# Attention and a squared-ReLU layer on one core: sums and copies placed on GpSimd, the last columns in one piece, and a new order

## The chip, the core and the metric

The kernel runs on one core of one Trainium2 chip. A core has TensorE (matmuls, into PSUM banks), VectorE, ScalarE and GpSimd (elementwise work; GpSimd also issues most of the loads) and SyncE (issues stores and transposing DMAs). Each engine works through its own list of instructions in order and waits on semaphores for the others. The metric is the time of one execution in device microseconds (us).

## The reference

The inputs are q, k and v with 4 batches, 8 heads, 768 positions and 64 columns each, and the weights w_in (512 x 2048) and w_out (2048 x 512).

```python
scores = scale * np.matmul(q, k.transpose(0, 1, 3, 2))
is_global = pos[None, :] < 8
is_local = (rel >= 0) & (rel < 96)          # rel = row - column
scores = scores - slopes[h] * dist          # dist: distance, 96 for a global far column
scores = np.where(is_global | is_local, scores, -1e9)
a = softmax(scores)                          # over the columns
x = np.matmul(a, v)                          # (4, 8, 768, 64) -> (3072, 512)
out = (np.maximum(x @ w_in, 0) ** 2) @ w_out # (3072, 512), float32
```

## The kernel before, in words

**Tiles.** The 3072 rows are 24 tiles j of 128 rows, six to a batch. Since a row sees only 96 columns back and the 8 global ones, tile j needs k and v of tiles j and j-1 only; the global rows are copied into 8 rows of tile j-1's k and v that the window does not reach (`gk.j`, `gv.j`: emit_gk at line 719, emit_gv at line 791; read by tile j+1). For each tile: load q, k, v; transpose q and k (`tr` on TensorE and `T` as its copy out of PSUM for the first 8 tiles, a transposing DMA from SyncE, also `T`, for the later ones); scores `sc`; `exp` on ScalarE; the product with the bias table `mul` on VectorE; `pv` (two halves); `norm` (reciprocal and product, VectorE); and the transpose of x, `xT`.

**Blocks.** Two tiles make one of 12 blocks of 256 rows. The first layer is done directly for blocks 0 and 1 (`s1`, then `relu` and `sq`). From block 2 on it is done with seven products instead of eight (`h.blk.g.p1` to `p7`, line 938; g is one of two halves of w_in's 2048 columns), which need sums of operands:

- `isum.i.g` (i 0 to 3, line 881): sums of parts of w_in, 128 x 1024, made once, by VectorE, and kept where the first q and k tiles lay. isum.1 reads isum.0; product p5 reads isum.0, p6 isum.1, p3 isum.2, p7 isum.3.
- `xs.blk.i` (i 0 to 2, line 905): sums of parts of xT, the first 128 x 512, the others 128 x 256, three for each block, by VectorE. xs.0 serves p5 and p7, xs.1 serves p6, xs.2 serves p4.
- `u` copies a running product out of PSUM, `c` adds it to another product in PSUM and applies the ReLU, `q` squares (lines 938 to 1030).

The second layer is done directly for block 0 (`s2.0.s.sub`) and with seven products from block 1 on (`s2.blk.p1.g` and so on, line 1202). These need `wsum.i.g` (line 1126: sums of parts of w_out, 128 x 1024, made once; wsum.1 reads wsum.0, wsum.3 reads wsum.1; product p5 reads wsum.0, p6 wsum.1, p7 wsum.2, p4 wsum.3) and `sum.blk.i` (line 1159: sums of the hidden layer). `part` copies a product out of PSUM, `o` adds the last ones (in fin, line 1272), `st` stores. In the last block the product p3 and its `o` are cut in two, 192 and 64 columns (line 1197), each part with a store of its own.

**Loads.** Loads of q, k, v and of the weights are issued by GpSimd (swdge, line 304; issue lines L307 and L311 in the profile). The first 6 tiles and all weights are `ld` words of the order (ld.win.s.c for w_in's piece s, ld.wout.s for w_out's). From tile 6 on, `load.j` issues v, q and k of tile j. A `gate.j` is a one-element memset on VectorE that collects the waits of VectorE's side for a load into a buffer used before. GpSimd's list holds nothing else but the iota at the start.

**The order.** It is not made by the program at run time: the string ORDER (line 57) lists every step by name, with its PSUM banks behind a colon and its engine behind `@` (A ScalarE, V VectorE). Plan.run takes the words one by one and emits each step, so that each engine's list is the order of its words. Costs and due times in the calls of plan.op are not used in the run.

```python
for word in ORDER.split():
    word, _, banks = word.partition(":")
    name, _, letter = word.partition("@")
    name, _, nth = name.partition("#")
    o = byname[name][int(nth or 1) - 1]
    o["engine"] = self.ENGINES[letter] if letter else next(iter(o["engines"]))
```

In this text a step's place on TensorE is told as the amount of TensorE work that stands in front of it in the order: the sum of its matmuls' start-to-start steps (a product `h` is 0.45 us, half a product `s2` 0.44), counted from the first transpose.

Of the kernel before, what the change touches and what calls it, by code (L numbers as in the profile page):

```python
# [22 lines left out]
class Plan:  # L23


    ENGINES = {"A": "ACT", "V": "DVE"}
# [31 lines left out]
tr.0.0:0 T.0.0@A tr.1.0:1 T.1.0@A bias.0.0:23 sc.0.0 exp.0.1.0 ld.q.1 ld.k.1 exp.0.0.0 tr.0.1:4 tr.1.1:5 ld.v.0  # L58
bias.1.0:6701 T.0.1@A ld.k.2 pv.0.1:3 pv.0.0:2 T.1.1@A sc.1.0 norm.0.0 exp.1.1.0 norm.0.1 ld.q.2 tr.1.2:4 gk.1@V
tr.0.2:5 exp.1.0.0 T.0.2@V bias.2.0:2375 T.1.2@A sc.2.0 E0.0 ld.v.1 exp.1.0.1 pv.1.0:6 exp.1.1.1 ld.q.3 tr.0.3:4  # L60
ld.k.3 E0.1 pv.1.1:0 exp.2.0.0 exp.2.1.1 norm.1.0 ld.v.2 exp.2.1.0 tr.1.3:1 T.1.3@A exp.2.0.1 ld.win.6.0 gv.1@V
trx.0:2 ld.q.4 norm.1.1 ld.k.4 T.0.3@V gk.2@V ones.6 pv.2.0:6 sc.3.0:5304 norm.2.0 pv.2.1:1 xT.0@V norm.2.1 trx.1:7
ld.v.3 tr.0.4:6 ld.win.3.0 trx.2:2 exp.3.1.1 ld.win.4.0 ld.q.5 xT.1@V s1.0.6:4 gk.3@V gv.2@V exp.3.1.0 tr.1.4:1
exp.3.0.0 mul.3.0 exp.3.0.1 mul.3.1 pv.3.0:3 T.1.4@V xT.2@V pv.3.1:7 T.0.4@A ld.k.5 norm.3.0 sc.4.0:5061 exp.4.0.0
exp.4.1.0 s1.0.3:2 s1.0.3#2 norm.3.1 trx.3:3 gv.3@V s1.0.4:5 exp.4.1.1 xT.3@V s1.1.6:7 ld.v.4 relu.0.6@A relu.0.4@V
ld.win.2.0 tr.1.5:0 mul.4.0 tr.0.5:1 exp.4.0.1 ld.win.2.1 sq.0.4@A s1.1.4:3 gk.4@V T.0.5@A pv.4.0:4 s1.0.2:6
ld.win.0.0 sq.0.6@V T.1.5@V relu.0.3@A sc.5.0:5102 relu.1.4@A mul.4.1 s1.0.2#2 pv.4.1:3 norm.4.0 exp.5.1.0 norm.4.1
ld.win.0.1 s1.0.2#3 exp.5.0.1 ld.v.5 gv.4@V s1.0.2#4 sq.1.4@V s1.0.0:4 s1.1.2:1 relu.1.2@A s1.0.0#2 trx.4:0 ld.win.5.0
exp.5.0.0 s1.0.0#3 s1.0.0#4 ld.win.7.0 ld.win.1.0 s1.1.0:3 gate.11 sq.0.3@V mul.5.0 exp.5.1.1 s1.1.3:1 mul.5.1
pv.5.0:5 xT.4@A pv.5.1:2 relu.0.0@V gate.9 s1.1.5:0 s1.0.7:4 load.6 norm.5.0 sq.1.2@A relu.1.3@A norm.5.1 relu.0.2@A  # L70
sq.0.2@A s1.0.1:1 isum.0.0 ld.wout.4 sq.0.0@A relu.0.7@V ld.wout.0 isum.3.1 sq.1.3@A ld.wout.1 ld.wout.2 sq.0.7@V
relu.1.5@A s1.0.1#2 trx.5:5 xT.5@A xs.2.0 h.2.1.p1:6 s1.1.7:2 tr.0.6:4 relu.0.1@A s1.1.1:0 T.0.6@V sq.0.1@A tr.1.6:5
sq.1.5@V relu.1.6@A ld.wout.3 ld.wout.5 relu.1.0@A ld.wout.7 h.2.0.p1:1 u.2.1.1@V relu.1.1@A ld.wout.6 sq.1.6@A
relu.1.7@A u.2.0.1@A sq.1.7@A sq.1.1@A gate.10 sq.1.0@A isum.3.0 h.2.0.p2:4 h.2.1.p2:7 isum.1.0 gate.12 load.8
s2.0.0.0:3 s2.0.0.1:0 load.7 s2.0.1.1 s1.0.5:2 relu.0.5@A xs.2.1 isum.0.1 isum.1.1 isum.2.1 s2.0.2.1 h.2.0.p6 s2.0.1.0
u.2.0.2@A c.2.1.c11 xs.2.2 sum.1.0 T.8 isum.2.0 s2.0.2.0 c.2.0.c11 sq.0.5@A s2.0.3.1 sum.1.2 h.2.1.p6 s2.0.4.1
h.2.0.p7 T.1.6@A s2.0.5.1 s2.0.3.0 wsum.0.0 s2.1.p2.0:7 wsum.0.1 u.2.1.2@A sum.1.1 h.2.0.p5:2 s2.0.6.1 h.2.1.p7
u.2.1.3@A h.2.1.p5:5 q.2.1.c11@V c.2.1.c22 gate.13 s2.0.4.0 u.2.0.3@A q.2.1.c22@A s2.0.5.0 c.2.0.c22 wsum.1.0 wsum.1.1
load.9 q.2.0.c11@A s2.1.p1.0:4 s2.0.7.1 h.2.0.p4 s2.1.p1.1 s2.0.6.0 o.0.1@A c.2.0.c21@A h.2.0.p3 q.2.0.c22@A
q.2.0.c21@A h.2.1.p4 wsum.2.0 s2.0.7.0 wsum.3.1 st.0.1 part.1.p1@A tr.0.7:0 h.2.1.p3 wsum.2.1 sum.1.3 o.0.0@A  # L80
c.2.1.c21@A s2.1.p6.0 c.2.1.c12 c.2.0.c12 s2.1.p6.1 T.0.7@A tr.1.7:1 part.1.p6@A q.2.1.c21@A T.1.7@V s2.1.p2.1
q.2.0.c12@A s2.1.p7.0 st.0.0 s2.1.p7.1 o.1.p2 q.2.1.c12@A sc.6.0:360521 load.10 wsum.3.0 part.1.p7@V s2.1.p5.0 gk.7@A
s2.1.p5.1 s2.1.p4.0 s2.1.p4.1 sum.2.0 exp.6.0.0 s2.2.p1.0:3 o.1.p5 exp.6.1.0 exp.7.0.0 o.1.p4@A mul.6.0 pv.6.1:6
pv.6.0:0 exp.7.1.0 exp.7.1.1 s2.1.p3.0 s2.2.p1.1 T.9 exp.7.0.1 sum.2.1 norm.6.0 load.11 mul.7.0 mul.7.1 norm.6.1
part.2.p1@A sc.8.0:4501 exp.8.0.0 s2.1.p3.1 pv.7.0:2 exp.8.1.1 norm.7.0 s2.2.p6.0 pv.7.1:4 norm.7.1 gk.8@V exp.8.1.0
gv.7@V trx.6:6 s2.2.p6.1 exp.8.0.1 xT.6@A s2.2.p2.0:1 mul.8.0 mul.8.1 trx.7:2 xT.7@A xs.3.0 o.1.p3 sc.9.0:5046
exp.9.0.0 s2.2.p2.1 h.3.0.p1:2 xs.3.1 exp.9.1.0 h.3.1.p1:5 sum.2.2 exp.9.0.1 pv.8.0:7 norm.8.0 xs.3.2 h.3.1.p2:0
u.3.1.1@A h.3.0.p2:4 h.3.1.p6 c.3.1.c11 u.3.0.1@A exp.9.1.1 o.2.p2 part.2.p6@A h.3.0.p5:7 c.3.0.c11 h.3.0.p6 pv.8.1:6
u.3.1.2@A load.12 mul.9.1 s2.2.p5.0 u.3.0.2@A gate.14 T.10 gv.8@A h.3.1.p7 q.3.0.c11@A norm.8.1 load.13 h.3.0.p7
u.3.0.3@A mul.9.0 pv.9.1:0 s2.2.p5.1 h.3.1.p5:4 pv.9.0:6 s2.2.p7.0 u.3.1.3@A st.1.0 q.3.1.c11@A s2.2.p7.1 c.3.0.c22  # L90
h.3.0.p3 part.2.p7@A norm.9.0 q.3.0.c22@A gv.9@V h.3.1.p4 c.3.1.c22 q.3.1.c22@A c.3.0.c12 h.3.1.p3 o.2.p5 c.3.1.c12
gk.9@V norm.9.1 s2.2.p4.0 c.3.1.c21@A h.3.0.p4 T.11 q.3.0.c12@A sum.2.3 q.3.1.c12@A s2.2.p4.1 sum.3.0 sc.10.0:6754
exp.10.0.0 gate.15 sum.3.1 s2.3.p1.0:0 s2.3.p1.1 s2.2.p3.0 exp.10.1.0 xT.8 mul.10.0 o.2.p4@A s2.2.p3.1 part.3.p1@A
sum.3.2 h.4.0.p1:6 exp.10.1.1 s2.3.p6.0 s2.3.p6.1 exp.10.0.1 mul.10.1 pv.10.0:7 part.3.p6@A T.12 xT.9 q.3.1.c21@A
norm.10.0 gk.10@V h.4.0.p2:3 u.4.0.1@A o.2.p3 pv.10.1:4 norm.10.1 s2.3.p7.0 c.3.0.c21@A s2.3.p7.1 st.1.1 xs.4.0
h.4.1.p1:5 sc.11.0:7124 xs.4.1 c.4.0.c11 q.3.0.c21@A h.4.0.p6 gv.10@V xs.4.2 u.4.1.1@A h.4.1.p6 exp.11.1.0 T.13
u.4.0.2@A s2.3.p2.0:3 u.4.1.2@A exp.11.1.1 s2.3.p2.1 xT.10 q.4.0.c11@V sum.3.3 o.3.p2 h.4.1.p2:1 c.4.1.c11 exp.11.0.0
exp.11.0.1 mul.11.0 h.4.0.p7 h.4.1.p7 u.4.0.3@A mul.11.1 h.4.0.p5:4 c.4.0.c22 q.4.1.c11@A h.4.1.p5:7 pv.11.0:1 st.2.0
s2.3.p5.0 u.4.1.3@A c.4.1.c22 norm.11.0 h.4.0.p4 pv.11.1:2 gate.16 part.3.p7@A s2.3.p5.1 h.4.1.p4 q.4.0.c22@A
q.4.1.c22@A c.4.1.c21@A s2.3.p4.0 norm.11.1 c.4.0.c21@A s2.3.p4.1 o.3.p5 h.4.0.p3 h.4.1.p3 xT.11 c.4.0.c12 s2.3.p3.0  # L100
o.3.p4@A s2.3.p3.1 q.4.1.c21@A load.15 c.4.1.c12 q.4.1.c12@A q.4.0.c12@V o.3.p3 q.4.0.c21@A sc.12.0:125604 exp.12.0.0
st.2.1 T.15 s2.4.p1.0:7 s2.4.p1.1 exp.13.0.0 load.14 sum.4.0 sum.4.1 xs.5.0 h.5.1.p1:3 h.5.0.p1:1 st.3.0 exp.12.1.0
h.5.1.p2:5 part.4.p1@A u.5.0.1@A u.5.1.1@A exp.13.1.0 xs.5.1 h.5.0.p2:2 mul.12.0 c.5.0.c11 s2.4.p6.0 h.5.0.p6
q.5.0.c11@A s2.4.p6.1 gk.13@A pv.12.0:2 pv.12.1:6 exp.13.1.1 c.5.1.c11 h.5.1.p6 h.5.0.p5:5 u.5.0.2@A part.4.p6@A
s2.4.p2.0:4 xs.5.2 s2.4.p2.1 u.5.1.2@A norm.12.0 exp.13.0.1 h.5.0.p7 mul.13.0 pv.13.0:2 u.5.0.3@A gate.18 norm.12.1
sum.4.2 mul.13.1 c.5.0.c22 q.5.1.c11@A h.5.1.p7 s2.4.p7.0 o.4.p2 h.5.1.p5:6 q.5.0.c22@A norm.13.0 gate.20 u.5.1.3@A
h.5.0.p4 h.5.0.p3 pv.13.1:0 s2.4.p7.1 c.5.0.c21@A h.5.1.p4 gv.13@A c.5.0.c12 T.14 norm.13.1 c.5.1.c22 s2.4.p5.0
q.5.0.c21@A sum.4.3 q.5.1.c22@V xT.12 s2.4.p5.1 gate.17 sc.14.0:2150 q.5.0.c12@A h.5.1.p3 part.4.p7@A c.5.1.c12
gk.14@V exp.14.0.0 exp.14.0.1 o.4.p5 exp.14.1.0 mul.14.0 s2.4.p4.0 exp.14.1.1 xT.13 s2.5.p1.0:2 h.6.0.p1:5 mul.14.1
q.5.1.c12@A s2.4.p4.1 o.4.p4@A s2.4.p3.0 c.5.1.c21@A sum.5.0 u.6.0.1@A xs.6.0 s2.4.p3.1 sc.15.0:6107 o.4.p3 load.16  # L110
xs.6.1 sum.5.1 h.6.1.p1:3 exp.15.1.1 s2.5.p1.1 exp.15.0.0 pv.14.0:4 norm.14.0 h.6.0.p6 pv.14.1:7 h.6.0.p5:6
part.5.p1@A s2.5.p6.0 s2.5.p6.1 exp.15.0.1 T.16 gate.21 q.5.1.c21@A gv.14@V u.6.0.2@A h.6.0.p2:0 h.6.0.p7 gk.15@V
u.6.1.1@A st.3.1 h.6.1.p6 load.18 mul.15.1 norm.14.1 exp.15.1.0 u.6.0.3@A xs.6.2 c.6.0.c11 sum.5.2 sc.16.0:4710
part.5.p6@V mul.15.0 h.6.0.p4 exp.16.0.0 s2.5.p7.0 c.6.0.c22 load.17 exp.16.1.0 s2.5.p7.1 pv.15.0:4 exp.16.0.1
c.6.0.c21@A part.5.p7@A mul.16.0 pv.15.1:7 exp.16.1.1 norm.15.0 s2.5.p2.0:1 s2.5.p2.1 o.5.p2 h.6.0.p3 norm.15.1
mul.16.1 q.6.0.c11@A c.6.0.c12 h.6.1.p2:5 s2.5.p4.0 u.6.1.2@A gv.15@A q.6.0.c21@A sum.5.3 st.4.0 xT.14 h.7.0.p1:4
h.7.1.p1:0 T.18 q.6.0.c22@A h.6.1.p7 u.6.1.3@A s2.5.p5.0 c.6.1.c11 gate.19 q.6.0.c12@A gk.16@A s2.5.p5.1 o.5.p5
h.6.1.p5:7 c.6.1.c22 s2.5.p4.1 pv.16.0:6 norm.16.0 pv.16.1:5 norm.16.1 h.6.1.p4 h.6.1.p3 c.6.1.c12 s2.5.p3.0 s2.5.p3.1
# [1309 lines left out]
```

## Time and profile before

| | us |
|---|---|
| median of three runs (198.21 to 198.69) | 198.6 |
| the profiled execution, whole | 198.07 |
| its span, from the first to the last instruction of the program | 196.3 |
| TensorE busy / VectorE / ScalarE / GpSimd | 189.2 / 172.4 / 162.9 / 75.1 |
| first matmul of the program's work (the transpose of tile 0) | 4.58 |
| last matmul's end | 192.93 |
| landing of the last store | 195.29 |

TensorE's granted clock is full throughout. Of the instructions' groups by line: L686 is `mul`, L774 and L775 `norm`, L884 `isum`, L918 `xs`, L946 `h`, L991 `c`, L1011 `q` on ScalarE, L1128 `wsum`, L1163 `sum`, L1208 `s2` from block 1 on, L1283 `o`, L1335 `s2` of block 0. L430 and L432 are the copies of ScalarE and of VectorE, whatever they copy. A line of the timeline has the start, the time from the first start to the last end, the engine, the line, the operation, output and inputs with their sizes, the count, and in brackets how long the engine had been idle and what ended it. A group's line has the busy time and the mean of one in ns, then the idle time before. GpSimd's DMA_DIRECT2D is the issue of a load, not its transfer.

### The profile page before, as it was taken

The numbers are of one execution on the slowest core, as the hardware profiler recorded it, in microseconds if no ns is written. First come the engines' busy times: TensorE is split into PE (matmuls) and PEld (weight loads), VectorE is DVE, ScalarE is ACT, GpSimd is POOL, SyncE is SP. The second block draws the span as 40 slices with busy tenths as digits, with TensorE's granted clock in tenths as the row PEclk, the third lists the DMA queues.
The fourth block names the chain that finished last, engine by engine and source line by source line (L and its number), as shares of the span: only waits on it lengthen the run. The fifth ranks groups of instructions, "written<-read, shape, count | busy, mean of one in ns | idle before, by whom it ended". The sixth has DMA issues, their size and how long they took to land.

```text
span 196.3 us, 6770 instructions
## 1 busy us (share of the span) xinstructions
PE 189.2 (96%) x2768; PEld 168.7 (86%) x2768; DVE 172.4 (88%) x426; ACT 162.9 (83%) x335; POOL 75.1 (38%) x93
## 2 busy tenths in 40 slices
PE   7897999999999999999999999999999999999993
PEld 3766999867889989989989999999888999999982
DVE  8188889999989999989999999998999989889772
ACT  6895879966989988979999999889787889878740
POOL 8998895665465309050542085054000000000000
PEclk9999999999999999999999999999999999999999
DMA  8999999999999999989999999999915242034032
GB/s 127 149 157 175 171 187 184 205 186 155 156 182 135 224 129 152 166 108 180 157 128 185 162 97 143 173 158 152 174 33 188 53 62 84 0 30 164 0 134 80
DMA packets 111856, 26.91 MB, mean 137 GB/s; under 512 B 103378, under 2 KB 109010, under 8 KB 111826
## 3 DMA queue, kind: packets, MB, share of 16 engines
q0 software_dynamic: 80256, 13.37, 90.0%
q1 hardware_dynamic: 31570, 13.11, 33.9%
q8 instruction: 21, 0.34, 0.7%
q14 instruction: 9, 0.07, 0.1%
HBM read 27.26 MB, written 6.29 MB: 171 GB/s over the span
## 4 chain that ended last, share of the span: by engine, by line
PE 89%; POOL 5%; DMA 4%; DVE 1%; issue 1%; DVEq 0%; POOLq 0%
PE bank L1208 34%; PE bank L946 32%; PE bank L1057 7%; PE bank L595 5%; PE bank L744 5%; DMA qk_first<-in_q_dram 4%; PE bank L1335 4%; POOL qk_first L307 3%; POOL v L307 1%; PE bank L505 1%; PE bank L812 1%; DVE at L686 0%; POOL win L307 0%; DVE o L1283 0%; POOL early L368 0%
## 5 line engine op out<-in xcount | busy, mean ns | idle before, releaser
L661 ACT ACTIVATE esc<-bank 128x512 bf16<-128x512 f32 x78 | 42.4, 608 | 5.0 <-PE bank L595 4.8
L1011 ACT ACTIVATE hs<-hr 128x512 bf16<-128x512 f32 x71 | 43.3, 635 | 2.5 <-DVE hr L991 1.8
L1208 PE MATMUL bank<-wsum,hsum 128*128 128x256 bf16 x264 | 36.2, 273 | 0.0
L991 DVE CUSTOM_DVE_ANT_0 hr<-bank,early 128x512 f32<-128x512 f32 x45 | 30.6, 687 | 5.2 <-PE bank L946 2.1
L1208 PEld LDWEIGHTS <-hsum 128*128 128x128 bf16 x360 | 32.2, 98 | 3.2
L946 PEld LDWEIGHTS <-qk_first 128*128 128x128 bf16 x480 | 29.4, 98 | 1.6
L946 PEld LDWEIGHTS <-win 128*128 128x128 bf16 x480 | 29.6, 98 | 1.0
L430 ACT COPY early<-bank 128x512 f32<-128x512 f32 x43 | 24.8, 594 | 6.0 <-PE bank L946 5.7
L311 POOL DMA_DIRECT2D v<-in_v_dram x18 | 15.9, 884 | 34.8 <-ACT hs L1011 13.2
L1208 PEld LDWEIGHTS <-hs 128*128 128x128 bf16 x264 | 24.5, 98 | 3.1
L686 DVE TENSOR_TENSOR at<-esc,E 128x1024 bf16<-128x1024 bf16 x39 | 26.1, 683 | 0.3 <-ACT esc L661 0.3
L1208 PE MATMUL bank<-wout,hs 128*128 128x256 bf16 x176 | 24.5, 273 | 0.0
L311 POOL DMA_DIRECT2D qk<-in_q_dram x18 | 15.9, 883 | 22.1 <-DMA qkT<-qk 16.8
L946 PE MATMUL bank<-xs,qk_first 128*128 128x128 bf16 x320 | 22.8, 219 | 0.0
L946 PE MATMUL bank<-xT,win 128*128 128x128 bf16 x320 | 22.6, 219 | 0.0
L775 DVE TENSOR_TENSOR x<-bank,rs 128x256 bf16<-128x256 f32 x48 | 20.4, 425 | 1.7
L861 ACT ACTIVATE hr<-bank 128x512 f32<-128x512 f32 x33 | 19.1, 598 | 2.1 <-PE bank L1057 1.3
L744 PE MATMUL bank<-v,at 128*128 128x65 bf16 x352 | 17.5, 193 | 0.3 <-DVE v L432 0.2
L1283 DVE TENSOR_TENSOR o<-bank,part 128x256 f32<-128x256 f32 (+2 forms) x34 | 14.0, 414 | 3.2 <-PE bank L1208 3.0
L311 POOL DMA_DIRECT2D qk<-in_k_dram x18 | 16.1, 892 | 1.0 <-DMA wout<-in_moe_w_out_dram 0.8
L744 PEld LDWEIGHTS <-at 128*128 128x128 bf16 x352 | 15.0, 98 | 1.7 <-DVE at L686 0.4
L1057 PE MATMUL bank<-xT,win 128*128 128x256 bf16 (+1 forms) x160 | 16.0, 251 | 0.0
(85 smaller groups left out, 340.9 us busy)
## 6 DMA issues: line engine op xcount, KB each, us to landing
out_dram<-o SPq DMA_DIRECT2D x22, 256.0 KB, 4.3
v<-in_v_dram POOLq DMA_DIRECT2D x24, 128.0 KB, 6.0
qk<-in_q_dram POOLq DMA_DIRECT2D x18, 128.0 KB, 6.0
qk<-in_k_dram POOLq DMA_DIRECT2D x18, 128.0 KB, 6.4
wout<-in_moe_w_out_dram POOLq DMA_DIRECT2D x8, 256.0 KB, 9.0
win<-in_moe_w_in_dram POOLq DMA_DIRECT2D x6, 256.0 KB, 6.9
qk_first<-in_q_dram POOLq DMA_DIRECT2D x5, 128.0 KB, 4.6
qk_first<-in_k_dram POOLq DMA_DIRECT2D x5, 128.0 KB, 4.6
```

Of the source, the lines that this page charges most:

```text
L311: nc.gpsimd.dma_start(out=dst, in_=src)
L430: nc.scalar.copy(dst, src)
L661: nc.scalar.activation(out=tiles[tag, j, g][:, odd], in_=tiles.pop(("sc", j, odd, g)).rearrange("p a c -> p (a c)"), func=Act.Exp, scale=s ...
L686: nc.vector.tensor_mul(at, tiles.pop(("esc", j, g)), bias)
L744: nc.tensor.matmul(out=po[:, hi, :], lhsT=tiles["at", j, g][:, odd, at * P : (at + 1) * P], rhs=v_sb[kj][:, h, :], start=(i == 0), stop=(i ...
L775: nc.vector.tensor_tensor(out=x[:, 4 * hf : 4 * hf + 4, :], in0=po[:, :, :D], in1=rs.to_broadcast([P, 4, D]), op=Alu.mult,)
L861: nc.scalar.activation(dst, src, Act.Relu)
L946: nc.tensor.matmul(out=tiles["h", blk, g, bank][:, n], lhsT=left_[:, s, k], rhs=right_[:, k], start=opens and n == 0 and k == 0, stop=k == ...
L991: nc.vector._custom_dve(TENSOR_ADD_SAT, out=hr, in0=src, in1=tiles.pop(("u", blk, g, i)), s0=float("inf"), s1=0.0,)
L1011: nc.scalar.activation(hs, hr, Act.Square)
L1057: nc.tensor.matmul(out=hT[:, c, cols], lhsT=w_in_sb[s][:, kt, c * P : (c + 1) * P], rhs=tiles["xT", blk][:, kt, cols], start=(kt == 0), st ...
L1208: nc.tensor.matmul(out=tiles["acc", blk, bank][:, cols], lhsT=left_[:, s], rhs=right_[:, cols], start=first and s == 0, stop=s == NSTEP - ...
```

## The change

A letter P for GpSimd is added. `isum`, `xs`, `wsum` and `gv` may be placed there. In the new ORDER isum.0.0, isum.0.1, wsum.0.1, wsum.1.1, wsum.2.0, wsum.2.1, 25 of the 30 xs and 10 of the 16 gv are (the other 6 gv are on ScalarE). VectorE keeps isum.1.x, 2.x and 3.x, wsum.0.0, 1.0, 3.0 and 3.1, and xs.2.0, 2.1, 7.0, 9.0 and 9.2. Some copies and squares change between ScalarE and VectorE: VectorE takes 8 more `part`, 7 more squares, 2 more `relu`, 3 more `u` and one more `xT`; ScalarE takes 3 more `gk`. The last block's p3 is no longer cut in two. All words of ORDER stand in a new sequence, the `ld` words too.

```diff
-    ENGINES = {"A": "ACT", "V": "DVE"}
+    ENGINES = {"A": "ACT", "V": "DVE", "P": "POOL"}
...
+    def tensors(e):
+        return nc.gpsimd if e == "POOL" else nc.vector
+
     def any_copy(e, dst, src):
         if e == "ACT":
             nc.scalar.copy(dst, src)
+        elif e == "POOL":
+            nc.gpsimd.tensor_copy(dst, src)
...
-                    nc.vector.tensor_tensor(out=first_sum[i][:, h], in0=x, in1=y, op=op)
+                    tensors(e).tensor_tensor(out=first_sum[i][:, h], in0=x, in1=y, op=op)
...
-                    ("isum", i, g), {"DVE": 0.6}, emit_isum,
+                    ("isum", i, g), {"DVE": 0.6, "POOL": 1.7}, emit_isum,
...
-            nc.vector.tensor_tensor(out=dst, in0=x, in1=y, op=Alu.subtract)
+            tensors(e).tensor_tensor(out=dst, in0=x, in1=y, op=Alu.subtract)
...
-                nc.vector.tensor_tensor(
+                tensors(e).tensor_tensor(
                     out=w_sum[i][:, h],
...
-            cuts = [slice(0, LASTCUT), slice(LASTCUT, HN)] if last and name == "p3" else [slice(0, HN)]
+            cuts = [slice(0, HN)]
```

The part of the new ORDER with the sums of the weights (the old one had all of them on VectorE):

```diff
+relu.0.3@A sc.5.0:7305 s1.0.2:1 ld.wout.0 ld.win.5.0 ld.wout.3 s1.0.2#2 ones.6 relu.1.4@V trx.4:6 sq.1.6@A s1.0.2#3
+sq.0.3@V ld.wout.1 relu.0.0@V s1.0.1:2 s1.0.2#4 xT.4@V exp.5.1.1 exp.5.0.1 ld.wout.2 mul.5.1 gv.4@A exp.5.1.0 load.6
+ld.wout.4 load.7 isum.0.0@P E0.1 h.2.0.p1:5 exp.5.0.0 mul.5.0 s1.0.1#2 s1.1.2:0 pv.5.1:6 pv.5.0:3 h.2.0.p2:7 sq.1.4@A
+sq.0.0@V relu.0.1@A s1.1.1:2 relu.1.2@V sq.0.1@A isum.0.1@P norm.5.0 ld.wout.5 ld.wout.6 sq.1.2@V relu.1.3@A sq.1.3@A
+s1.1.7:0 s1.1.5:4 u.2.0.1@A relu.1.1@A relu.1.5@A relu.0.2@V norm.5.1 gate.10 gate.9 sq.1.1@V h.2.1.p1:3 h.2.1.p2:1
+trx.5:2 xT.5@A sq.1.5@A isum.3.0@V c.2.0.c11 isum.1.0@V u.2.1.1@A s2.0.0.0:6 s2.0.0.1:4 xs.2.0@V q.2.0.c11@A sq.0.2@A
+xs.2.1@V s2.0.1.1 s1.1.0:7 relu.1.0@A ld.wout.7 wsum.2.0@P s2.0.1.0 isum.1.1@V h.2.0.p6 u.2.0.2@A sq.1.0@A c.2.1.c11
...
+h.2.0.p4 h.2.1.p7 c.2.0.c21@A h.2.1.p5:7 s2.0.5.1 q.2.0.c22@A wsum.0.1@P wsum.1.1@P q.2.0.c21@V u.2.1.3@A wsum.2.1@P
...
+c.2.1.c21@A o.0.1@A sum.1.3 T.1.7@A s2.0.5.0 q.2.1.c22@V h.2.1.p3 T.0.7@A c.2.1.c12 wsum.3.1@V s2.0.6.0 s2.0.7.0
+s2.1.p1.0:2 s2.1.p1.1 sc.6.0:034571 o.0.0@A s2.1.p2.0:6 s2.1.p2.1 q.2.1.c12@A part.1.p1@A s2.1.p6.0 s2.1.p6.1
+q.2.1.c21@A load.10 sum.1.2 sum.2.0 exp.6.0.0 exp.6.1.0 exp.7.0.1 exp.7.1.1 s2.2.p1.0:0 mul.6.0 pv.6.1:3 s2.2.p1.1
```

The loads in the order of their issue, before and after (w is a piece of w_in, o of w_out; w0 and w2 come in two halves; a number stands for q, k or v of that tile; from 6 on a `load` is v, q, k):

```
before: q1 k1 v0 k2 q2 v1 q3 k3 v2 w6 q4 k4 v3 w3 w4 q5 k5 v4 w2 w2 w0 w0 v5 w5 w7 w1 load.6 o4 o0 o1 o2 o3 o5 o7 o6 load.8 load.7 load.9
after:  q1 k1 q2 k3 k2 q3 v0 v1 w6 v2 k4 q4 v3 w3 w4 q5 k5 v4 w0 w0 w2 w2 w1 w7 v5 [gv.3] o0 w5 o3 o1 o2 load.6 o4 load.7
        [isum.0.0] [isum.0.1] o5 o6 o7 [wsum.2.0] [xs.2.2] load.8 load.9 [wsum.0.1] [wsum.1.1] [wsum.2.1] load.10 load.11 [xs.3.0] ...
```

## The prediction, as it was put on record

> **What bounds it now.** I read the page's busy shares and slices first, then the chain of waits, then TensorE's matmuls one by one, then the waits and the timeline of GpSimd.
>
> ```profile
> PE 189.2 (96%) x2768; PEld 168.7 (86%) x2768; DVE 172.4 (88%) x426; ACT 162.9 (83%) x335; POOL 75.1 (38%) x93
> PE   7897999999999999999999999999999999999993
> POOL 8998895665465309050542085054000000000000
> PE 89%; POOL 5%; DMA 4%; DVE 1%; issue 1%; DVEq 0%; POOLq 0%
> ```
>
> TensorE is below nine tenths only in the first four slices and the last; the chain that ended last is 89% TensorE. Laid end to end by their start-to-start steps, the matmuls after 17.1 us leave one hole over 0.2 us (0.24 at 140.4). So the time is TensorE's work plus the hole in front of it plus the tail; GpSimd is idle for most of the span, but it issues all loads. The change takes no TensorE work away (eight matmuls of 192 and eight of 64 columns become eight of 256: 0.02 us). It can gain only before 17 us, at the tail, and at that hole. It can lose wherever TensorE comes to wait.
>
> VectorE is near its limit at 30 to 60 us (9.28, 9.41 and 9.30 us busy in each ten), so a wait there is hardly made good.
>
> **The loads.** The timeline of GpSimd at 28 to 38 us carries the most:
>
> ```profile
> 28.72 0.70 POOL L307 DMA_DIRECT2D wout<-in_moe_w_out_dram  x1 [0.32 <-DMA win<-in_moe_w_in_dram]
> 30.05 0.71 POOL L307 DMA_DIRECT2D wout<-in_moe_w_out_dram  x1 [0.63 <-DMA win<-in_moe_w_in_dram]
> 31.90 0.70 POOL L307 DMA_DIRECT2D wout<-in_moe_w_out_dram  x1 [1.14 <-DMA win<-in_moe_w_in_dram]
> ...
> 35.62 0.87 POOL L311 DMA_DIRECT2D v<-in_v_dram  x1 [0.61 <-DMA wout<-in_moe_w_out_dram]
> 36.87 0.87 POOL L311 DMA_DIRECT2D qk<-in_q_dram  x1 [0.38 <-DMA wout<-in_moe_w_out_dram]
> 38.15 0.87 POOL L311 DMA_DIRECT2D qk<-in_k_dram  x1 [0.41 <-DMA wout<-in_moe_w_out_dram]
> ```
>
> These issues wait for a transfer: load n is issued 0.28 us after load n-8 has landed (28.43 then 28.72, 35.33 then 35.62). The program has eight semaphores for such loads, and the changed program waits for them in the same way. Landings are evenly spaced: about 0.85 us for a piece of q, k or v, 1.3 for a weight piece of 256 KB, 0.7 for a half piece. The first 22 loads are the same set in both kernels, in another order, so the 22nd lands at 26.28 in both. From there the changed list gives win 1 27.6, win 7 28.9, v5 29.8, wout 0 31.1, win 5 32.4, wout 3 33.7, wout 1 35.0.
>
> *First loads: -0.2.* Only the first 17 us have holes, and loads 1 to 22 bring no more by then. In the changed order s1.0.1 stands after 18.8 us of TensorE work and needs win 1 (27.6). Before, TensorE had that much work behind it at 27.85. Gain at most 0.2, whatever the first tiles save.
>
> **Two sums of w_in on GpSimd: +1.75.** GpSimd works in order. isum.0.0 stands behind load.7, its k piece the 37th load, which waits for the 29th (wout 1, 35.0): issue 35.25, done 36.13 (0.88 as in the rows above). Only then can the sum begin. VectorE's isum.1.0 needs it and comes up in VectorE's order after 25.9 us of TensorE work (34 to 36 us); xs.2.0 and xs.2.1 queue behind it there; TensorE's h.2.0.p6 needs all three.
>
> A sum on GpSimd is not in this trace. Nearest rows:
>
> ```profile
> L884 DVE TENSOR_TENSOR qk_first<-win 128x1024 bf16<-128x1024 bf16 x2 | 1.4, 682 | 0.0
> L918 DVE TENSOR_TENSOR xs<-xT,xs 128x256 bf16<-128x256 bf16 x20 | 5.7, 284 | 0.3
> L918 DVE TENSOR_TENSOR xs<-xT 128x512 bf16<-128x512 bf16 x10 | 4.2, 416 | 0.0
> L432 DVE COPY v<-v 8x520 bf16<-8x520 bf16 x11 | 3.5, 322 | 0.0
> L368 POOL IOTA early<- 128x256 int32 x1 | 0.3, 333 | 0.4 <-POOLq L1409 0.4
> ```
>
> From below VectorE's 0.68 us. GpSimd's only computing row, the iota, takes 1.30 ns a column for one stream: 1.33 us for 1024 columns, 2.66 if the two operands are read one after the other; that is my upper end. I take 2.0, the middle of GpSimd's own two; for 512 and 256 columns 1.0 and 0.65, for the copy of v 0.7.
>
> isum.0.0 then ends at 38.1, and isum.1.0 (0.62 apart when back to back), xs.2.0 (0.36) and xs.2.1 (0.28) at 39.4. h.2.0.p6 stands after 28.5 us of TensorE work; before, that was reached at 37.65. TensorE is 1.75 us behind (the 0.2 is in this); with 0.68 it is 0.4, with 2.66 it is 2.4.
>
> (The Trainium skill, GPSIMD Engine Reference, section "Performance versus the Vector engine", gives 4497 ns for 2048 float32 columns. Half of it, 2.25 us as an estimate for 1024, would make this term 2.0 and the next 1.7. No run here shows it yet.)
>
> **Four sums of w_out on GpSimd: +1.05.** On GpSimd follow isum.0.1 (to 40.1), three wout issues (0.71 each, 42.3), wsum.2.0 (44.3), xs.2.2 (44.9), load.8 and load.9 (six by 0.88, 50.2), wsum.0.1 (52.2), wsum.1.1 (54.2). VectorE, which also waited for isum.0.1 until 40.1, has 13.9 us by rows from there to wsum.3.1, 12.7 at its back-to-back pace: it arrives at 52.8 and waits for wsum.1.1 until 54.2. Behind it stand sum.1.2, sum.2.0 and mul.6.0, which ends 2.5 us later, at 56.7. TensorE comes to pv.6.1 16.25 us after h.2.0.p6, at 55.65, and stalls 1.05. At 1.7 a sum this is nothing; at 2.66 it is 3.9.
>
> **Twenty-five sums of x: +0.3.** GpSimd makes the pair xs.0 and xs.1 in 1.65 instead of 0.70, 0.95 more. Before, the pair was ready 0.12 to 0.34 us ahead of product p6 in blocks 4, 6, 7 and 11. The new order moves p6 away from the last pv of its block: 8.0 us of TensorE work instead of 6.2 in block 11, 8.5 for 7.0 in 6, 9.4 for 8.5 in 7, 9.2 for 7.4 in 5, 10.7 for 8.9 in 10. That covers it, except in block 4 (8.5 for 9.8) and block 9 (7.6 for 7.4). In block 8 load.21, which waits for the transpose of tile 18, stands ahead of xs.8.0. I put 0.3 on all; between nothing and 2.
>
> **Ten copies of v: 0.** A pv of tile j and the next tile's pv that reads the copy stand at least 1.7 us of TensorE work apart (tile 20); GpSimd needs 0.7, 1.4 if it reads and writes in turn. What would lie late then is pv.21.0.
>
> **Moves between ScalarE and VectorE: 0.** By the rows VectorE loses 16.7 us (25 xs 8.0, six sums 4.1, eleven v copies 3.5, three k copies 0.9, the split 0.2) and takes 12.0 (8 part, 7 squares, 2 relu, 3 u, one xT); ScalarE loses 10.1. Both stay below TensorE. They hid before behind 100% TensorE and do so now; if not, the first to be late are the `c` sums, which left p3 0.13 us.
>
> **The last 256 columns: -0.2.** Now 192 columns are added in 0.36 (192.97), 64 more by 193.46, and two stores go out at 193.35 and 193.78, the last landing at 195.29. One addition of 0.42 ends at 193.4, one store follows and takes 1.65 to 1.75 as its like do: 195.1.
>
> **The sum.** 1.75 + 1.05 + 0.3 - 0.2 = +2.9. On the profiled execution (198.07, span 196.3) that is 201.0. The three runs shown have their median at 198.6, 0.5 above it, so I forecast **201.5**.
>
> **Rivals.**
>
> *The port.* One row speaks of GpSimd and VectorE in each other's way:
>
> ```profile
> 14.10 1.02 POOL L307 DMA_DIRECT2D qk_first<-in_q_dram  x1
> 14.40 0.72 DVE L432 COPY qkT<-qkT 128x32 bf16<-128x32 bf16 x1
> 17.09 0.17 DVE L432 COPY qkT<-qkT 128x32 bf16<-128x32 bf16 x1
> ```
>
> The held copy ends when the GpSimd issue does (15.12); alone it takes 0.17. VectorE's additions of two SBUF operands (0.67 to 0.69 in all 39 `mul` products) are not held by issues. If GpSimd's sums hold those, GpSimd's 12 us of large sums and 19 us of xs each keep VectorE from its two-operand work, 80 of its 168 us. At 30 to 60 us, where VectorE is 93% busy, some 4 us of it reach TensorE, and a little in each block: 206. Against it: no row shows it. (The Trainium skill, SBUF — State Buffer, section "Who interferes with whom", says this: a VectorE instruction with two SBUF inputs contends with a GpSimd one that reads SBUF, the loser waiting to the end. The held copy agrees with its rule for copies; its rule for sums no run here shows.)
>
> *Short sums.* At 0.7 to 1.2 us TensorE is behind by 0.4 to 0.9 only, and the tail takes back 0.2: 199.0.
>
> *Faster.* isum.0.0 is done before VectorE asks for it. It decides at 36.3: then h.2.0.p6 has its operands by 37.65. The last issue ahead would have to end near 34.3, so wout 1 land at 33.1, not 35.0, and wsum.1.1 be done by 53. Then only gains stay: 0.2 first loads, 0.2 tail, 0.2 hole at 140 us: 197.5, as a median 198.0. For it speaks that VectorE is freed of 4.7 us; against it the steady spacing of landings.
>
> *The reordered loads bring nothing*: they land no earlier for the work that needs them. At 0.2 us this is already in the sum.
>
> **Chances.** Forecast 0.50 (200 to 204), port 0.17, short sums 0.11, faster 0.16, no difference (the gains and half a stall cancel) 0.06. A measurement tells some 0.3% (0.6 us) apart: faster 0.16, same 0.06, slower 0.78. Sums at 2.66 give 205 to 206; the range 198.5 to 206 leaves out the faster case and some of the port's.
>
> **What would show it.** isum.0.0 starts at 36 us and VectorE idles before isum.1.0, released by GpSimd; TensorE has a hole of 1.5 to 2 us before h.2.0.p6 near 38 us and one near 56; a dense TensorE after 60. Wrong, if no hole stands near 38 us, if the GpSimd sums last under 1.3 us or over 2.7, if VectorE's `mul` products last longer than 0.69, or if holes gather later, ahead of p6.

## The result, and the profile after

The changed kernel takes 220.12 us (median; 217.53 to 225.54), the kernel before 198.41 on the same chips: ratio 1.107, 95% interval 1.103 to 1.111. The ratio leaves out the one run in the slow state, 225.54. The profiled execution of the changed kernel took 219.96 us with a span of 218.2, against 196.3 before. Line numbers after are 4 higher than before from `exp` on (L690 is `mul`, L888 `isum`, L922 `xs`, L950 `h`, L1017 `q` on VectorE, L1132 `wsum`, L1167 `sum`), and one lower for the loads (L306, L310).

The page of the changed kernel: busy times, the slices of TensorE, of GpSimd and of TensorE's clock, and the chain by engine.

```profile
PE 195.5 (90%) x2760; PEld 170.9 (78%) x2760; DVE 188.5 (86%) x402; ACT 155.6 (71%) x317; POOL 119.5 (55%) x134
PE   7989998079289999979989899998999999999993
POOL 8998958997971077195186476808641126021000
PEclk9999999658969999999999999999999999999999
PE 51%; DVE 17%; POOL 13%; DMA 13%; issue 3%; ACT 1%; DVEq 0%; POOLq 0%
```

TensorE's row has two deep breaks, at slices 8 and 11 (a slice is 5.5 us), and shallow ones later; the clock's row drops in the deep ones and just behind them. The chain is only half TensorE now. VectorE was to lose 4.7 us of work by its rows and shows 16.1 us more.

TensorE's own timeline, around the two breaks (in brackets: how long it had been idle, and what ended that):

```profile
36.98 0.59 PE L1339 MATMUL bank<-wout,hs 128*128 128x512 bf16 x2
44.97 1.86 PE L950 MATMUL bank<-xs,qk_first 128*128 128x128 bf16 x16 [7.39 <-DVE xs L922]
...
61.01 1.01 PE L950 MATMUL bank<-xT,qk_first 128*128 128x128 bf16 x8 [5.18 <-DVE hr L995]
```

The first is h.2.0.p6, where the forecast had a hole of 1.75 us; it is 7.39. The second is h.2.0.p3. VectorE's timeline says why:

```profile
34.89 0.68 DVE L995 CUSTOM_DVE_ANT_0 hr<-bank,early 128x512 f32<-128x512 f32 x1
38.35 4.11 DVE L888 TENSOR_TENSOR qk_first<-qk_first,win 128x1024 bf16<-128x1024 bf16 x1 [2.78 <-POOL qk_first L888]
42.38 0.41 DVE L922 TENSOR_TENSOR xs<-xT 128x512 bf16<-128x512 bf16 x1
42.83 2.08 DVE L922 TENSOR_TENSOR xs<-xT,xs 128x256 bf16<-128x256 bf16 x1
...
51.73 3.58 DVE L1167 TENSOR_TENSOR hsum<-hs 128x1024 bf16<-128x1024 bf16 x1 [0.91 <-ACT hs L1098]
55.34 2.49 DVE L1167 TENSOR_TENSOR hsum<-hsum,hs 128x1024 bf16<-128x1024 bf16 x1
57.75 2.60 DVE L1132 TENSOR_TENSOR wsum<-wout,wsum 128x1024 bf16<-128x1024 bf16 x1
```

isum.1.0 begins at 38.35, when isum.0.0 is there, as foreseen. Then it lasts 4.11 us instead of 0.68, and xs.2.1 lasts 2.08 instead of 0.28. The three sums at 51.73 to 60.35 take 2.5 to 3.6 us each; TensorE's second wait is for the `c` that stands behind them on VectorE. These five take 14.9 us; alone they take 3.0. GpSimd's timeline beside them:

```profile
35.29 0.88 POOL L310 DMA_DIRECT2D qk<-in_k_dram  x1 [0.40 <-DMA wout<-in_moe_w_out_dram]
36.18 4.20 POOL L888 TENSOR_TENSOR qk_first<-win 128x1024 bf16<-128x1024 bf16 x2
40.32 2.16 POOL L306 DMA_DIRECT2D wout<-in_moe_w_out_dram  x3
42.50 2.26 POOL L1132 TENSOR_TENSOR wsum<-wout 128x1024 bf16<-128x1024 bf16 x1
...
52.60 2.15 POOL L1132 TENSOR_TENSOR wsum<-wout 128x1024 bf16<-128x1024 bf16 x1
54.82 2.46 POOL L1132 TENSOR_TENSOR wsum<-wout,wsum 128x1024 bf16<-128x1024 bf16 x1
```

Each long VectorE sum lies over a GpSimd sum. Four of the five end shortly behind its end: xs.2.1 at 44.91, 0.15 us behind wsum.2.0 (44.76); the sum of 51.73 at 55.30, 0.56 behind wsum.0.1 (54.74); the two after it 0.55 behind the next two. The fifth, isum.1.0, ends 2.08 us behind isum.0.1; the last section comes back to it. Operations that read PSUM (`c`, `norm`, `o`) lie over GpSimd sums too and keep their 0.68, 0.42 and 0.42 us.

What GpSimd's work itself takes, in its groups (busy us, mean ns of one, idle before):

```profile
L922 POOL TENSOR_TENSOR xs<-xT,xs 128x256 bf16<-128x256 bf16 x18 | 15.5, 860 | 3.8 <-DVE xs L922 1.9 <-DVE rs L778 0.8
L434 POOL COPY v<-v 8x520 bf16<-8x520 bf16 x10 | 6.4, 639 | 15.3 <-PE bank L748 15.3
L888 POOL TENSOR_TENSOR qk_first<-win 128x1024 bf16<-128x1024 bf16 x2 | 4.2, 2128 | 0.0
```

Where TensorE lost 22 us, by its starts against the work ahead of them in the order: 7.4 in the first break, 2.6 at half clock behind it, 5.3 in the second, 1.7 at half clock behind that, 5.0 spread over blocks 3 to 11; 0.2 was gained before 30 us.

### The profile page after: what moved, and what is told of

It reads as the page before. It is cut to its first block, busy times and chain, and to the rows that moved or that the text cites. A ratio compares the mean times of both kernels' runs of the same rounds, so it can differ in the third digit from the quotient of the medians.

```text
span 218.2 us, 6750 instructions
## 1 busy us (share of the span) xinstructions
PE 195.5 (90%) x2760; PEld 170.9 (78%) x2760; DVE 188.5 (86%) x402; ACT 155.6 (71%) x317; POOL 119.5 (55%) x134
## 4 chain that ended last, share of the span: by engine, by line
PE 51%; DVE 17%; POOL 13%; DMA 13%; issue 3%; ACT 1%; DVEq 0%; POOLq 0%
PE bank L1212 23%; PE bank L950 20%; DMA xT<-x 6%; DVE hsum L1167 5%; DMA wout<-in_moe_w_out_dram 4%; POOL qk_first L306 3%; POOL xs L922 3%; DMA win<-in_moe_w_in_dram 3%; PE bank L599 3%; PE bank L748 3%; PE bank L1339 2%; DVE hr L995 2%; POOL v L306 2%; DVE at L690 2%; DVE qk_first L888 2%
## 5 line engine op out<-in xcount | busy, mean ns | idle before, releaser
L1015 ACT ACTIVATE hs<-hr 128x512 bf16<-128x512 f32 x65 | 40.2, 637 | 12.5 <-DVE hr L995 12.4
L950 PEld LDWEIGHTS <-qk_first 128*128 128x128 bf16 x480 | 31.0, 100 | 18.2 <-issue 11.6
L1212 PE MATMUL bank<-wsum,hsum 128*128 128x256 bf16 x264 | 37.5, 273 | 0.7 <-ACT early L432 0.7
L432 ACT COPY early<-bank 128x512 f32<-128x512 f32 x39 | 22.5, 585 | 17.2 <-PE bank L950 16.8
L950 PE MATMUL bank<-xs,qk_first 128*128 128x128 bf16 x320 | 24.2, 223 | 10.5 <-DVE xs L922 7.4
L922 POOL TENSOR_TENSOR xs<-xT 128x512 bf16<-128x512 bf16 x7 | 9.1, 1294 | 42.9 <-DMA xT<-x 21.6
L950 PEld LDWEIGHTS <-win 128*128 128x128 bf16 x480 | 29.8, 98 | 1.6 <-ACT early L432 0.3
L690 DVE TENSOR_TENSOR at<-esc,E 128x1024 bf16<-128x1024 bf16 x39 | 27.5, 716 | 2.4 <-ACT esc L665 2.2
L950 PE MATMUL bank<-xT,win 128*128 128x128 bf16 x320 | 23.1, 219 | 0.0
L1167 DVE TENSOR_TENSOR hsum<-hs 128x1024 bf16<-128x1024 bf16 (+1 forms) x24 | 19.5, 821 | 1.5 <-ACT hs L1098 0.9
L310 POOL DMA_DIRECT2D v<-in_v_dram x18 | 16.3, 906 | 8.2 <-DVE hsum L1167 6.1
L310 POOL DMA_DIRECT2D qk<-in_q_dram x18 | 16.1, 892 | 3.7 <-DMA qkT<-qk 1.8
L922 POOL TENSOR_TENSOR xs<-xT,xs 128x256 bf16<-128x256 bf16 x18 | 15.5, 860 | 3.8 <-DVE xs L922 1.9
L950 PE MATMUL bank<-xT,qk_first 128*128 128x128 bf16 x160 | 12.4, 223 | 5.2 <-DVE hr L995 5.2
```

Of the source, the lines that this page charges most:

```text
L310: nc.gpsimd.dma_start(out=dst, in_=src)
L432: nc.scalar.copy(dst, src)
L690: nc.vector.tensor_mul(at, tiles.pop(("esc", j, g)), bias)
L922: tensors(e).tensor_tensor(out=dst, in0=x, in1=y, op=Alu.subtract)
L950: nc.tensor.matmul(out=tiles["h", blk, g, bank][:, n], lhsT=left_[:, s, k], rhs=right_[:, k], start=opens and n == 0 and k == 0, stop=k == ...
L1015: nc.scalar.activation(hs, hr, Act.Square)
```

## The experiments

**Theory A**, formed from these lines: while GpSimd makes a sum, VectorE's instructions with two SBUF operands stand still; TensorE waits for them, and the long waits cost it its clock too. **Theory B**, the forecast's: TensorE waits because GpSimd's results come late. **Theory C**: the new sequence and the moves between ScalarE and VectorE cost it, wherever the sums are made. Each kernel ran beside the kernel before on one chip.

**All of GpSimd's steps on VectorE (e1_all_v).**

```diff
-isum.0.0@P ... xs.3.0@P ... gv.9@P (41 words)
+isum.0.0@V ... xs.3.0@V ... gv.9@V
```

> The changed kernel with all 41 steps of GpSimd given to VectorE, at their places in the order: the new order, loads and last piece alone. Theory A (VectorE's instructions with two SBUF operands are held while GpSimd's sums run, and TensorE's two long waits that follow also cost it its clock): without sums on GpSimd no VectorE sum lasts over 0.75 us, the holes before h.2.0.p6 (7.4 us) and h.2.0.p3 (5.2 us) go, the granted clock is 1.000 throughout; VectorE has 12 us more work than before, which may cost a little: 198 to 202 us. Theory B (the forecast's: TensorE waits because GpSimd makes the sums late, in its queue behind the loads): also 198 to 202, since no one waits for GpSimd; but VectorE's sums were never held. Theory C (the new order itself is bad, whoever makes the sums): above 212, with long holes at the same steps.

Measured: 211.32 us, 1.068 of before (1.062 to 1.074). All sums are back at 0.68 us and both breaks are gone, but the time is far above what A and B expected; nor is it C's, which had it above 212 with long holes at the same steps. The waits of TensorE, the largest first:

```profile
PE bank L1212 <- DVE o L1287: 2.2, 1, 2.2
PE bank L950 <- DVE hr L995: 2.0, 2, 1.4
```

With the start's 1.2 us it waits 9.6 us in all for VectorE, in short waits. VectorE has 182.4 us of work here, 10.0 more than before; by this run's rows 15.6 of it are the steps put back (25 xs 8.1, six sums 4.1, ten copies 3.4).

**Only the weights' sums (e2_weights_v), or only the xs (e3_xs_v), back on VectorE.**

```diff
-isum.0.0@P isum.0.1@P wsum.2.0@P wsum.0.1@P wsum.1.1@P wsum.2.1@P
+isum.0.0@V isum.0.1@V wsum.2.0@V wsum.0.1@V wsum.1.1@V wsum.2.1@V
```

> The changed kernel with only the 6 sums of weights back on VectorE; 25 xs and 10 gv stay on GpSimd. From the trace of the changed kernel TensorE loses 12.7 us in the two holes and 4 us at half clock behind them, and 5 us from block 3 on. Theory A: both holes and the half clock go, the 5 us from block 3 on stay: 202 to 206 us, clock 1.000; VectorE sums met by a GpSimd xs still last 0.8 to 1.7 us. Theory B: only the forecast's 0.3 for the xs stays: 198 to 199.5. Theory C: above 212.

Measured: 209.68 us, 1.058 (1.054 to 1.062). The breaks are gone. VectorE's sum at 64.5 us, over an xs on GpSimd, still lasts 1.60. The time is 3.7 us more than A's upper end, and the clock is 0.992, not 1.000. VectorE has the 4.1 us of these sums to do in its fullest stretch; that this is the reason is likely but not shown.

```diff
-xs.2.2@P xs.3.0@P ... (25 words)
+xs.2.2@V xs.3.0@V ...
```

> The changed kernel with only the 25 xs back on VectorE; the 6 sums of weights and 10 gv stay on GpSimd. Theory A: the two holes and the half clock before 65 us stay (17 us), the 5 us from block 3 on go: 213 to 217 us, and VectorE has sums of 2.5 to 4 us at 38 to 60 us and none over 0.75 after that. Theory B (the xs cost 0.3): 219 to 221.

Measured: 225.37 us, 1.126 (1.117 to 1.136), slower than the change itself. Both expectations missed. The weights' breaks stay (7.4 and 5.2 us), and the xs on VectorE cost more than they did on GpSimd, holding and all. So taking steps back from GpSimd measures two things at once: the holding that goes, and the work that VectorE gets.

**Sums on GpSimd that no one waits for (e4_before_10_unread_sums).** In the kernel before, behind load.23:

```diff
+                if j == NT - 1:
+                    for _ in range(10):
+                        nc.gpsimd.tensor_tensor(
+                            out=dup, in0=w_out_all[:, :4, 1, HN:], in1=w_out_all[:, :4, 0, HN:], op=Alu.subtract)
```

> The kernel before, with ten sums of 128 x 1024 of w_out on GpSimd behind its last load (137.6 us), into a buffer that no one reads: GpSimd's work without anyone waiting for its result, and without a load behind it. Theory A (VectorE's two-SBUF-operand instructions are held until the GpSimd sum that they meet ends): the sums run from 138 to about 160 us, each holds VectorE for 0.5 to 2.0 us, so VectorE loses some 13 of 22 us there and TensorE most of that: 206 to 213 us; mul, sum, q and xs in that stretch last up to 2.7 us, c, norm and o (an operand in PSUM) as long as before. Theory B (only the wait for GpSimd's results costs): 198.4 within 0.6, all VectorE rows as before.

Measured: 212.58 us, 1.072 (1.065 to 1.078), in A's range, where B expected no change. VectorE's timeline in this run, with the ten sums on GpSimd from 137.51 to 162.63 (ends at 139.66, 142.19, 144.73, ...):

```profile
138.39 1.83 DVE L1018 TENSOR_TENSOR hs<-hr 128x512 bf16<-128x512 f32 x1
140.35 0.69 DVE L996 CUSTOM_DVE_ANT_0 hr<-bank,u 128x512 f32<-128x512 f32 x1
140.96 1.78 DVE L691 TENSOR_TENSOR at<-esc,E 128x1024 bf16<-128x1024 bf16 x1
...
143.35 0.42 DVE L780 TENSOR_TENSOR x<-bank,rs 128x256 bf16<-128x256 f32 x1
```

`q` and `mul` end at 140.22 and 142.75, 0.55 us behind the GpSimd sums that they met; `c` and `norm`, with an operand in PSUM, take what they always take. This is holding without any dependency.

**The same place, other work of GpSimd.** Twenty memsets (no read of SBUF; e8_before_20_memsets), or ten copies (one read; e12_before_10_copies), in place of the ten sums:

```diff
+                    for _ in range(20):
+                        nc.gpsimd.memset(dup, 1.0)
```

> The kernel before with twenty memsets of 128 x 1024 bf16 on GpSimd behind its last load, at the place of the ten unread sums of e4_before_10_unread_sums (212.6 us): GpSimd is as busy, writes SBUF, and reads nothing from it. If what holds VectorE is GpSimd's reading (the Trainium skill, SBUF — State Buffer, section "Who interferes with whom", says that two-input VectorE instructions contend only with a GpSimd instruction that reads SBUF): 198.1 within 0.8, mul, sum, q and xs as long as before, at most the short copies held. If any work on GpSimd holds VectorE: 203 to 213 us.

Measured: 198.65 us, 1.002 (1.001 to 1.004). The groups of this run at 137 to 164 us (`mul`), and over the run (memset):

```profile
L690 DVE TENSOR_TENSOR at<-esc,E 128x1024 bf16<-128x1024 bf16 x9 | 6.1, 682 | 0.0
L478 POOL MEMSET dup<- 128x1024 bf16 x20 | 19.1, 957 | 1.1
```

Nineteen us of writing leave `mul` at 0.68; only two copies of v, 0.28 us alone, were held, to 0.60 and 0.96.

```diff
+                    for _ in range(10):
+                        nc.gpsimd.tensor_copy(dup, w_out_all[:, :4, 1, HN:])
```

> The kernel before with ten copies of 128 x 1024 bf16 from w_out into a spare buffer on GpSimd behind its last load: one operand read from SBUF, where e4_before_10_unread_sums read two (212.6 us) and e8_before_20_memsets none (198.7). At the 0.64 us of the changed kernel's copies of 520 columns, a copy lasts some 1.3 us, the ten 13 us. If any reading by GpSimd holds VectorE's two-operand instructions: mul, sum and q that meet a copy last up to 1.8 us, some 6 us of VectorE lost, 201 to 206 us. If only two reads hold it: 198.2 to 198.9, as with the memsets.

Measured: 201.77 us, 1.022 (1.015 to 1.028).

```profile
L690 DVE TENSOR_TENSOR at<-esc,E 128x1024 bf16<-128x1024 bf16 x8 | 7.4, 934 | 0.0
L478 POOL COPY dup<-wout 128x1024 bf16<-128x1024 bf16 x10 | 13.4, 1340 | 0.6
```

One operand read from SBUF is enough: `mul` is at 0.93 in the mean, up to 1.52. (So the rule of the Trainium skill, SBUF — State Buffer, section "Who interferes with whom", holds here as it is written: two SBUF inputs on VectorE against a GpSimd instruction that reads SBUF, not one that only writes.)

**Is it the sequence or the engines (e5_new_sequence_old_engines, e6_old_sequence_new_engines)?**

```diff
-relu.1.4@V ... part.2.p1@V ... xs.3.0@P ...   (the change's letters, in its sequence)
+relu.1.4@A ... part.2.p1@A ... xs.3.0 ...     (the letters of before, in the new sequence)
```

> The changed kernel's sequence of steps (and its loads and last piece), but every step on the engine that it has in the kernel before: nothing on GpSimd, VectorE 172 us and ScalarE 163 us by the rows. With all steps of GpSimd on VectorE (e1_all_v, 211.3 us) VectorE had 182 us of work and was the one that TensorE waited for. Theory A2 (those 13 us come from the 12 us of copies and squares that moved from ScalarE to VectorE, which make VectorE the bound): 198 to 202 us. Theory C (the sequence itself costs them): 207 us or more.

Measured: 221.38 us, 1.117 (1.114 to 1.120). The explanation that the 13 us of the first experiment come from the moves to VectorE falls: undoing them makes it worse, with 13.4 us of waits of TensorE for VectorE and 7.3 for ScalarE. C's range, 207 or more, is met: with the engines of before, the new sequence is dear by itself.

```diff
-xs.3.0 ... gv.9@V ... part.2.p1@A   (the letters of before, in its sequence)
+xs.3.0@P ... gv.9@P ... part.2.p1@V (the change's letters, in the old sequence)
```

> The sequence of the kernel before, with every step on the engine that the change gives it: 6 sums of weights, 25 xs and 10 gv on GpSimd, the moves between ScalarE and VectorE too, last 256 columns in one piece. Theory A (GpSimd's sums hold VectorE's two-operand instructions and TensorE loses its clock behind long waits): 210 to 225 us, sums of 2 to 4 us on VectorE at 30 to 60 us. Theory C (the new sequence is what costs): 198 to 203 us.

Measured: 254.13 us, 1.281 (1.277 to 1.285), more than A expected too, and far from C's 198 to 203. Each sequence goes with its own engines; neither half of the change can be judged by grafting it onto the other kernel. That left open what the change as a whole would cost without the holding.

**The change without GpSimd's reading (e9_no_reads_on_gpsimd).** Every wait stays, and the durations nearly; the sums themselves are left out. `corner` is two columns of each operand:

```diff
+    def stand_in(out, in0, in1, op, pad):
...
+        nc.gpsimd.tensor_tensor(out=out[corner], in0=in0[corner], in1=in1[corner], op=op)
+        nc.gpsimd.memset(pad, 0.0)
+        nc.gpsimd.memset(out, 0.0)
...
-                    tensors(e).tensor_tensor(out=first_sum[i][:, h], in0=x, in1=y, op=op)
+                    if e == "POOL":
+                        stand_in(first_sum[i][:, h], x, y, op, dup)
...
```

> The changed kernel, order and engines as they are, with each of the 31 sums on GpSimd replaced by a sum of two columns (which keeps every wait for its operands) and two memsets, one into a spare buffer and one into the sum's own place, about as long as the sum: 2 x 0.96 us for 1024 columns. The sums themselves are left out, so that the output is not the reference's; the ten copies of v stay. GpSimd's results come as late as before, but GpSimd hardly reads SBUF. Theory A (the holding of VectorE, and the clock lost behind the long waits it makes, are what the change costs): no VectorE sum over 0.9 us, holes of 1 to 2 us where the changed kernel has 7.4 and 5.2, clock 1.000: 199 to 204 us, the forecast's 201.5 in it. Theory B (the lateness of GpSimd's results): 215 to 221. Theory C (the new sequence and the moves between ScalarE and VectorE, by which e1_all_v is at 211.3): 208 to 213.

Measured: 203.08 us, 1.023 (1.019 to 1.027); clock 1.000. B and C fall as the explanation of the 21.7 us. VectorE's and TensorE's timelines of this run:

```profile
35.08 0.68 DVE L1010 CUSTOM_DVE_ANT_0 hr<-bank,early 128x512 f32<-128x512 f32 x1
38.13 0.69 DVE L900 TENSOR_TENSOR qk_first<-qk_first,win 128x1024 bf16<-128x1024 bf16 x1 [2.36 <-POOL qk_first L246]
...
55.68 0.69 DVE L1151 TENSOR_TENSOR wsum<-wout,wsum 128x1024 bf16<-128x1024 bf16 x1 [3.31 <-POOL wsum L246]
```

```profile
39.53 1.05 PE L965 MATMUL bank<-xs,qk_first 128*128 128x128 bf16 x16 [1.81 <-DVE xs L937]
...
55.70 0.60 PE L1226 MATMUL bank<-wsum,hsum 128*128 128x256 bf16 x4 [0.66 <-POOL wsum L246]
...
58.24 0.29 PE L757 MATMUL bank<-v,at 128*128 128x65 bf16 x4 [1.50 <-DVE at L699]
```

GpSimd's first result comes at the same time as in the changed kernel (isum.0.0's at 38.1, there 38.3), wsum.1.1's at 55.65 instead of 57.28, since there GpSimd's sums were held too. isum.1.0 takes 0.69 instead of 4.11, and TensorE's wait before h.2.0.p6 is 1.81 instead of 7.39. By this run the reading, with the lost clock that follows from it, costs 220.1 - 203.1 = 17.0 of the 21.7 us. Of the other 4.6, the waits for late results shown here are 1.81 + 0.66 + 1.50 = 4.0: that much of B is true.

The same stand-in for the weights' sums alone, and then for the xs alone:

> The same stand-in for the 6 sums of weights alone (their sums are left out); the 25 xs and 10 gv on GpSimd as in the changed kernel. Theory A: the two long holes and the half clock go, 13 to 17 us, the 5 us from block 3 on stay: 203 to 207 us. Theory B: 215 to 221.

Measured: 208.38 us, 1.053 (1.046 to 1.060), clock 1.000: the reading of the 6 weights' sums costs 11.7 us; the time is 1.4 us over A's upper end.

> The same stand-in for the 25 xs alone (those sums are left out); the 6 sums of weights on GpSimd as in the changed kernel. Theory A: the holes at 37 and 55 us and the half clock stay, the 5 us from block 3 on go: 213 to 217 us. Theory B: 219 to 221.

Measured: 213.43 us, 1.074 (1.071 to 1.078); the time is in A's range, and the first break stays at 7.5 us. The reading of the 25 xs costs 6.7 by this run, which is rough: the second break is 2.7 us instead of 5.2, as only two of the three sums in it are held, and in its profile an early wait of 1.8 us for a load of v, with half clock behind it, costs some 1.5 us that the changed kernel does not lose. The two together give 18.4, near the 17.0.

**The last columns (e7_before_one_piece).** The kernel before with only `cuts = [slice(0, HN)]`:

> The kernel before with only its last 256 columns in one piece. The forecast's term: 0.2 us less, 197.9; it would be nothing, or 0.1 to 0.3 more, if the landing of the last store waits for its size and not for its issue.

Measured: 198.01 us against 198.17, ratio 1.000 (0.999 to 1.001). In the traces the last store lands at 195.23 instead of 195.29: the one addition ends at 193.52, not at the 193.4 of the forecast, since TensorE's last matmul ends 0.13 us later. No version here beats the kernel before.

## Why the prediction was wrong

Slower was right, and the rival that names the cause stood in it, at 206 us and a chance of 0.17. What failed, step by step:

- **The loads and GpSimd's queue: right.** The landings of win 5, wout 3 and wout 1 were put at 32.4, 33.7 and 35.0 and came at 32.76, 33.72 and 35.00; isum.0.0 was put at 36.13 and began at 36.18. In part this is luck: the 22nd load landed at 25.52 and not at 26.28, and those after it up to wout 0 0.7 to 0.8 early as well; then win 5 came 2.43 us behind wout 0, where 1.3 was put, and the two errors cancelled.
- **The price of a sum on GpSimd: right.** 2.0 us was taken; the two isum take 2.13 in the mean. For xs 1.0 and 0.65 were taken, and the shortest are 1.15 and 0.66 (the means, 1.29 and 0.86, have their own waits in them); the copy of v 0.7, measured 0.64. (The estimate of 2.25 us by the Trainium skill, GPSIMD Engine Reference, section "Performance versus the Vector engine", is as near to 2.13 as mine.)
- **The step that failed: "isum.1.0 (0.62 apart when back to back), xs.2.0 (0.36) and xs.2.1 (0.28) at 39.4".** It priced VectorE's sums by rows in which GpSimd never computes. They took until 44.91, because isum.0.1 and wsum.2.0 ran beside them (what the three issues between these two added is open, see the last section). So +1.75 became 7.4. Without GpSimd's reading the wait is 1.81: the step's sum was right for that case.
- **Four sums of w_out, +1.05:** the second break is 5.2 us, at h.2.0.p3, ahead of pv.6.1, from the same cause. Without reading, TensorE waits 0.66 + 1.50 = 2.2 there: twice the forecast, since the stand-in of wsum.1.1 ends at 55.65, not 54.2. (By the prediction's own sum, its other figure here, 1.7 for sums of 2.25 us, comes out as 2.1.)
- **The xs, +0.3:** mis-sized. Their reading alone costs some 6.7 us. The term asked only whether the xs come in time, not whom they hold: sums, `mul` and `q` of 0.8 to 1.7 us from 77 us on.
- **"A dense TensorE after 60":** wrong. The signs named against the forecast came true: `mul` of up to 1.15 us, and holes ahead of p6 (TensorE waits 3.1 us in three of them, in blocks 4, 6 and 8, for an xs of GpSimd; 0.6 without reads).
- **The copies of v, 0:** TensorE waits 0.4 us for one. In the changed kernel's trace no sum of VectorE with two SBUF operands begins under one of them, so there they held none; what else they cost was not tried alone.
- **Moves between ScalarE and VectorE, 0:** not shown on its own. The run without reads has the moves in it, and TensorE is busy for 94% of it; undone in the new sequence, with nothing on GpSimd, the time rises from 211.3 to 221.4 us.
- **Last columns, -0.2:** 0.05 by the traces; the ratio, good to some 0.3 us, shows no difference.
- **First loads, -0.2:** TensorE was 0.2 us ahead at 30 us, as put.
- **Not in the forecast at all: the clock**, 2.6 + 1.7 us at half speed behind the two long breaks.
- **The port rival** had the mechanism and the place; its price failed. It let 4 us of VectorE's loss at 30 to 60 us reach TensorE. VectorE lost 11.9 there (14.9 for 3.0), and 8.6 of it reached TensorE (7.39 for 1.81 in the first break, 5.18 for 2.16 in the second), because the held sums are those that TensorE waits for next; and the clock came on top. "Against it: no row shows it" was no evidence: GpSimd computes nothing in the trace of before, so no row could.

## What to carry to other kernels

Before moving elementwise work to GpSimd, ask what it reads: in these runs, nearly every two-SBUF-operand instruction of VectorE that began under a GpSimd sum or copy out of SBUF stood until that ended, so the price is paid by VectorE's next sum more than by GpSimd. Place such work only where VectorE works out of PSUM, or give GpSimd writes alone (even these held two of VectorE's copies, by 0.3 and 0.7 us). Where a trace cannot show a contention because one party is idle in it, the rival needs the full price on the chain, and a stand-in with the same waits and durations but without the reads measures it in one run.

## What the runs showed of the hardware that was not expected

- A held VectorE sum ends 0.55 us behind the GpSimd instruction that held it (0.15 for the xs of 0.28), as if it had done about 0.13 us when it stops. The holding goes both ways: alternating with VectorE's sums, GpSimd's sum takes 2.45 us instead of 2.15, its copy 1.38 instead of 1.05.
- isum.1.0 ended 2.08 us behind the GpSimd sum that it met, at the end of three issues that followed (42.46 and 42.48), and it does the same in the traces of e3_xs_v and e11_xs_no_reads. The sum of 51.73 began under an issue and still waited for the GpSimd sum behind it; in e11_xs_no_reads one that began under an issue at the same place, at 52.11, took 0.69. Issues alone hold no such sum: in the trace of before, 15 `mul` begin under one and last 0.67 to 0.69. How an issue next to a GpSimd sum lengthens the wait was not tried and stays open.
- The clock falls to half in spells of one length or its multiples, read in steps of a quarter us: 3.5 us at 60.5 in the changed kernel and 10.5 at 40.0 (three times); 3.5 in the first two experiments each (at 110.0 and 82.0), behind waits of only 2.2 and 2.1 us. A wait of 2.5 us in the new sequence with the old engines brought none. (The Trainium skill, TensorE: Matmul & The Clock Gate, section "Part 1: The HAM clock gate (the "warmup" mystery)", has a free-running window of 3413 ns; the lengths agree. It gives an idle window of about 3.4 us as what throttles; here shorter waits sufficed.)
